# Loading a batch's rows ahead of one expert's weights, and adding masks on TensorE, in a fused attention and expert-mixture kernel

## The chip, the cores and the metric

One core of one Trainium2 chip. The metric is the device time of one execution in microseconds (us). Ratios are the mean time of one kernel's fast runs over the mean of the other's fast runs of the same rounds, so they are not quite the ratio of the medians quoted beside them. A ratio under 1 is faster than the kernel before. Brackets are 95% intervals.

## The reference

```python
# q, k, v: (4 batches, 8 heads, 768 positions, 64); 4 sink positions, window 128
keep = (pos_k < 4) | ((pos_q - pos_k >= 0) & (pos_q - pos_k < 128))
a = softmax(where(keep, q @ k.T / 8, -1e9));  attn = a @ v          # per head
x = attn, heads side by side                                        # (3072, 512)
p = probs / probs.sum(-1)                                           # 4 experts
out = sum_e p[:, e] * (relu(x @ w1[e]) @ w2[e])                     # w1 512x1024, w2 1024x512
```

## The kernel before

The program fixes the order of each engine's instructions beforehand. It keeps a small model of every engine's clock and of the DMA queues (`t`, `landed`, `turned_at`, `xT_at`) and always issues what the model says is ready next. Its figures are the program's own assumptions. So a number in the model moves instructions, and a wrong number puts an instruction that isn't ready in front of others that are.

Row and weight loads go through GpSimd's software DMA queue. They convert float32 to bfloat16 on the way. Transposes are DMAs too, on SyncE's hardware queue. `turn_nat` turns a batch's q and k rows into `qkT` for the scores. `values` turns the attention output `onat` into `xT`, the input of the expert layers.

```python
def sp(*deps, issue=530, takes=600):             # the model of a hardware-queue DMA
    t["sp"] = max([t["sp"], *deps]) + issue
    at = max(t["hw"], t["sp"] + 800)
    t["hw"] = at + takes + max(0.0, min(takes, t["sw"] - at))   # at most twice as long
    return t["hw"] + 900                                        # beside software loads
# ... cut: turn_nat, where the margin (LATE = 2500) is added
turned_at[b, tb] = sp(landed["qk", b, tb], ..., issue=1330, takes=1400) + LATE
# ... cut: values(), batches 1 to 3
nc.sync.dma_start(out=xT[b, g]..., in_=o..., transpose=True)
turned_out = sp(at, issue=1330, takes=1400)
for x in range(NHP):
    xT_at[b, x, g] = turned_out                  # from here on T may be formed
# ... cut: tokens(): four sums T on VectorE from xT, for experts in a seven-product form
```

The first batch's scores are masked in one of two ways. A group below `BIASED` gets a product `ident x low` on TensorE that adds 0 or -32768 ahead of the scores. Any other group has the exponentials multiplied by a 0/1 mask on VectorE (L657).

When the first batch's attention is planned, the rest of the loads are queued: expert 3's first weights, the second batch's rows and values, expert 3's second weights. After a batch's last row transpose GpSimd runs a copy of two columns (`held`), which keeps the next batch's loads from overwriting rows that are still being turned.

The softmax here doesn't subtract the row's maximum and nothing guards it: scores larger than these inputs give would overflow.

## Time and profile before

| | |
|---|---|
| time | 370.87 us, median of 3 runs (370.61 to 371.45) |
| span of the profiled run | 368.9 us |
| TensorE busy | 358.5 us (97%) |
| largest wait of TensorE | 2.47 us, sink scores of the second batch on a row transpose, at 78.4 us |
| granted clock, 79 to 83 us | 0.57 |

In the profile PE is TensorE, DVE VectorE, ACT ScalarE, POOL GpSimd and SP SyncE, and L12 is line 12 of the kernel. A line of a timeline has the start, the duration, the engine, the line, the operation with its tiles, and in brackets how long the engine had idled before it and what ended that.

### The profile page before, as it was taken

How to read it: one execution, taken by the hardware profiler on the slowest of the kernel's cores; microseconds unless marked ns; L12 is line 12 of the kernel's file. 1: busy time of each engine (PE TensorE's matmuls, PEld its weight loads, DVE VectorE, ACT ScalarE, POOL GpSimd, SP SyncE). 2: the span in 40 equal slices, each digit the busy share in tenths (PEclk: the TensorE clock that was granted, in tenths of full speed). 3: DMA queues.
4: the chain of work that ended last, by engine and by line, in shares of the span. 5: the costliest groups of instructions: out<-in, count | busy, mean ns of one | idle time of the engine just before them, and what ended most of it. 6: DMA issues, size and time to landing. Idle time of an engine off the chain costs nothing.

```text
span 368.9 us, 9862 instructions
## 1 busy us (share of the span) xinstructions
PE 358.5 (97%) x4105; PEld 296.9 (81%) x4117; DVE 283.1 (77%) x629; ACT 154.7 (42%) x397; POOL 71.2 (19%) x92
## 2 busy tenths in 40 slices
PE   7899999979999999999999999999999999999996
PEld 3585767637677788898888898899999999999995
DVE  6855985636662899779969979869898988898860
ACT  5854633566556245446445545552103213223110
POOL 8945117304900950010020000000000000000000
PEclk9999999989999999999999999999999999999999
DMA  9999999999999992519692031213002111020011
GB/s 164 172 187 200 210 206 146 148 161 136 137 182 210 200 165 43 85 45 88 129 157 76 15 103 30 44 44 85 16 17 87 30 44 59 16 74 2 2 59 57
DMA packets 117288, 37.20 MB, mean 101 GB/s; under 512 B 100612, under 2 KB 112740, under 8 KB 117244
## 3 DMA queue, kind: packets, MB, share of 16 engines
q0 software_dynamic: 77520, 17.31, 53.5%
q1 hardware_dynamic: 38668, 18.75, 24.6%
q8 instruction: 32, 0.52, 0.6%
q10 hardware_dynamic: 1056, 0.52, 0.5%
q14 instruction: 12, 0.10, 0.1%
HBM read 40.45 MB, written 6.34 MB: 127 GB/s over the span
## 4 chain that ended last, share of the span: by engine, by line
PE 74%; DMA 16%; POOL 4%; DVE 3%; issue 1%; ACT 0%; POOLq 0%; DVEq 0%; SPq 0%
PE acc L1235 29%; PE cps L1081 20%; PE hps L1003 15%; DMA w<-in_moe_w_dram 11%; PE acc L1306 6%; DMA qkT<-qkn 3%; DMA qkn<-in_k_dram 3%; PE sps L623 2%; PE od L689 2%; POOL qkn L191 1%; POOL vx L256 1%; PE od L682 1%; DVE H L1027 1%; POOL w L269 0%; POOL w L279 0%
## 5 line engine op out<-in xcount | busy, mean ns | idle before, releaser
L1003 PE MATMUL hps<-xT,w 128*128 128x256 bf16 x768 | 95.0, 273 | 0.8 <-DMA w<-in_moe_w_dram 0.7
L1003 PEld LDWEIGHTS <-w 128*128 128x128 bf16 x768 | 72.7, 98 | 13.7 <-issue 1.6
L1235 PEld LDWEIGHTS <-H 128*128 128x128 bf16 x600 | 56.0, 98 | 6.4 <-issue 0.8
L648 ACT ACTIVATE aT<-sps 128x512 bf16<-128x512 f32 (+1 forms) x96 | 47.2, 570 | 25.2 <-PE sps L623 25.1
L1081 PEld LDWEIGHTS <-w 128*128 128x128 bf16 x768 | 48.3, 98 | 2.0 <-issue 0.5
L1235 PE MATMUL acc<-w,H 128*128 128x256 bf16 x360 | 48.0, 273 | 0.0
L728 ACT ACTIVATE onat<-od,R 128x64 bf16<-128x64 f32 x144 | 33.4, 322 | 32.1 <-DVE R L716 30.2
L1306 PE MATMUL acc<-w,H 128*128 128x512 bf16 x180 | 45.3, 388 | 0.8 <-issue 0.3
L1100 DVE SCALAR_TENSOR_TENSOR H<-cps,gates 128x512 bf16<-128x512 f32 x57 | 38.6, 683 | 2.2 <-PE cps L1081 1.2
L1016 ACT ACTIVATE H<-hps 128x512 bf16<-128x512 f32 x40 | 23.9, 597 | 35.8 <-PE hps L1003 35.5
L1278 ACT COPY osb<-acc 128x256 f32<-128x256 f32 x36 | 13.5, 374 | 58.2 <-PE acc L1235 56.0
L1027 DVE SCALAR_TENSOR_TENSOR H<-hps,gates 128x512 bf16<-128x512 f32 x44 | 30.0, 685 | 9.3 <-PE hps L1003 9.1
L1306 PEld LDWEIGHTS <-H 128*128 128x128 bf16 x192 | 18.1, 99 | 18.7 <-issue 1.6
L256 POOL DMA_DIRECT2D vx<-in_v_dram x24 | 21.4, 910 | 58.8 <-PE od L689 51.9
L1235 PE MATMUL acc<-wf,H 128*128 128x256 bf16 x240 | 31.9, 273 | 0.0
L1235 PEld LDWEIGHTS <-S 128*128 128x128 bf16 x288 | 27.0, 98 | 3.1 <-issue 0.3
L1081 PE MATMUL cps<-T,w 128*128 128x128 bf16 x384 | 29.3, 219 | 0.0
L1081 PE MATMUL cps<-xT,w 128*128 128x128 bf16 x384 | 29.1, 219 | 0.0
L642 DVE TENSOR_TENSOR aT<-aT,mask 128x1024 bf16<-128x1024 bf16 (+1 forms) x36 | 22.6, 638 | 8.4 <-ACT aT L648 8.4
L1109 ACT COPY cps<-cps 128x512 f32<-128x512 f32 x24 | 13.8, 576 | 33.2 <-PE cps L1081 31.0
L1081 PEld LDWEIGHTS <-vf 128*128 128x128 bf16 x432 | 26.9, 98 | 1.0 <-issue 0.3
L1318 DVE SCALAR_TENSOR_TENSOR osb<-acc,scale_t,osb 128x512 f32<-128x512 f32 x18 | 13.5, 749 | 12.9 <-PE acc L1306 12.0
(116 smaller groups left out, 513.6 us busy)
## 6 DMA issues: line engine op xcount, KB each, us to landing
w<-in_moe_w_dram POOLq DMA_DIRECT2D x7, 1024.0 KB, 16.3
out_dram<-osb SPq DMA_DIRECT2D x23, 256.0 KB
gates<-gate_rows SPq DMA_DIRECT2D x36, 128.0 KB
vx<-in_v_dram POOLq DMA_DIRECT2D x24, 128.0 KB, 7.9
qkn<-in_q_dram POOLq DMA_DIRECT2D x22, 128.0 KB, 7.1
qkn<-in_k_dram POOLq DMA_DIRECT2D x22, 128.0 KB, 7.0
w<-in_moe_w_dram POOLq DMA_DIRECT2D x2, 512.0 KB, 8.1
kraw<-in_k_dram ACTq DMA_DIRECT2D x2, 256.0 KB
```

The lines of the kernel that those rows point to most:

```text
L256: nc.gpsimd.dma_start(out=vx[tb][:, :, 0:D], in_=v[b, :, tb * P:(tb + 1) * P, :].rearrange("h p d -> p h d"),)
L642: nc.vector.tensor_mul(a, a, m[:, None, :].to_broadcast([P, 2, w]))
L648: nc.scalar.activation(out=a[:, ph], in_=sps[ph][:, 0:w], func=AF.Exp, scale=scale)
L728: nc.scalar.mul(o[:, qi, hp, ph * D:(ph + 1) * D], od[:, qi, ph, 0:D], R[:, qi, ph])
L1003: nc.tensor.matmul(h[:, i].rearrange("p (q n) -> p q n", q=2), lhsT=w1_sb[e][:, db, fb * P:(fb + 1) * P], rhs=xT[b, g][:, :, db], start=(i ...
L1016: nc.scalar.activation(out=dst, in_=h, func=AF.Relu)
L1027: nc.vector.scalar_tensor_tensor(out=dst, in0=h, scalar=0.0, in1=gate, op0=ALU.max, op1=ALU.mult,)
L1081: nc.tensor.matmul(y[:, f], lhsT=A[:, d, f * P:(f + 1) * P], rhs=T[:, d], start=(m in ("P1", "P5") and f == 0 and d == 0), stop=(d == 1), ...
L1100: nc.vector.scalar_tensor_tensor(out=dst, in0=src, scalar=0.0, in1=gate, op0=ALU.max, op1=ALU.mult)
L1109: nc.scalar.copy(out=tiles["Y"], in_=y)
L1235: nc.tensor.matmul(x, lhsT=self.operand(b, g, e, m)[:, f], rhs=forms[e][m][:, f], start=(k == 0 and f == 0 and m in (("P1", "P5", "P2") if ...
L1306: nc.tensor.matmul(op, lhsT=H[:, fb // QF, fb % QF, s], rhs=w2_sb[e][:, fb, :], start=(fb == 0), stop=(fb == NFB - 1),)
```

## The change

The intent: the second batch's rows arrive one weight load earlier, and the model assumes that their transposes arrive much later, so that TensorE isn't sent to scores whose transposes are still under way. The masks of the first batch's second group of queries leave VectorE, which is nearly full there; the first group's are products already, and the third group's stay on VectorE.

```diff
-    BIASED = 1
+    BIASED = 2
...
-        turned_at[b, tb] = sp(...) + LATE
+        turned_at[b, tb] = sp(...) + (LATE if b > 1 else 8500)
...
-            loads.append((load_w1, 3))
             for tb in range(NQB):
                 loads.append((load_nat, 1, tb))
                 if tb % 2:
                     loads += [(load_v, 1, (tb - 1,)), (load_v, 1, (tb,))]
-            loads.append((load_w2, 3))
+            loads += [(load_w1, 3), (load_w2, 3)]
```

More of the change, by code (lines that the diff above doesn't have):

```diff
@@ L206, in turn_nat @@
         )
-        turned_at[b, tb] = sp(landed["qk", b, tb], scored_at.get(b - 1, 0.0), issue=1330, takes=1400) + LATE
+        turned_at[b, tb] = sp(landed["qk", b, tb], scored_at.get(b - 1, 0.0), issue=1330, takes=1400) + (LATE if b > 1 else 8500)
         qkn_free.remove(1e12)
```

## The prediction

> **What bounds the kernel now.** I read the page first: which engine is full, and when.
>
> ```profile
> PE 358.5 (97%) x4105; PEld 296.9 (81%) x4117; DVE 283.1 (77%) x629; ACT 154.7 (42%) x397; POOL 71.2 (19%) x92
> ...
> PE   7899999979999999999999999999999999999996
> ...
> PEclk9999999989999999999999999999999999999999
> DMA  9999999999999992519692031213002111020011
> ```
>
> TensorE is the bound almost throughout. Two slices matter: near 74 us PE drops to 7, and just after it, near 80 us, the granted clock drops to 8. DMA is full until about 70 us. So one event at 74 to 83 us costs time, and everything after it is a full TensorE, which passes a gain or a loss on to the end. The second view, waits on TensorE, names what is waited for:
>
> ```profile
> PE sinks L584 <- DMA qkT<-qkn: 2.5, 1, 2.5
> PE acc L496 <- DVE lent L410: 1.4, 1, 1.4
> PE hps L1003 <- DMA w<-in_moe_w_dram: 0.7, 2, 0.5
> PE sps L623 <- DVE qkT L227: 0.4, 1, 0.4
> ```
>
> The largest is one wait of 2.5 us by the second batch's sink scores for a transpose of its rows. The third view, the TensorE timeline around it (start, duration, line, and the idle time before), shows what follows the wait:
>
> ```profile
> 67.52 1.89 PE L1306 MATMUL acc<-w,H 128*128 128x512 bf16 x8
> ...
> 75.25 0.71 PE L689 MATMUL od<-vx,aT 128*128 128x65 bf16 x18
> 78.43 0.29 PE L584 MATMUL sinks<-qkT,ksd 128*32 128x256 bf16 x4 [2.47 <-DMA qkT<-qkn]
> 78.66 0.40 PE L623 MATMUL sps<-qkT 64*128 64x128 bf16 x6
> 78.98 3.21 PE L1306 MATMUL acc<-w,H 128*128 128x512 bf16 x8
> ```
>
> The same eight 512-column products take 1.89 us before the hole and 3.21 us after it. The stretches give the clock (window, its length, PE busy, ..., granted clock, DMA share, GB/s):
>
> ```profile
> 79.00:83.00 4.00, 4.00 (x23) 1.54 (x21) 1.44 (x2) 3.81 (x16) 0.00 (x0) 0.57 1.25 198
> 83.00:90.00 7.00, 6.95 (x82) 5.32 (x80) 3.95 (x8) 5.29 (x15) 1.91 (x3) 1.00 0.93 146
> ```
>
> So 4.00 x (1 - 0.57) = 1.7 us more is lost to a slower clock. The hole costs 2.5 + 1.7 = 4.2 us. Its origin is in the chain of work that ended last, in order of time, and in GpSimd's timeline:
>
> ```profile
> 28.99 27.61 DMA w<-in_moe_w_dram
> ...
> 58.79 9.38 DMA qkn<-in_k_dram
> 68.23 10.07 DMA qkT<-qkn
> ```
>
> ```profile
> 51.75 0.87 POOL L191 DMA_DIRECT2D qkn<-in_q_dram  x1 [4.17 <-DMA w<-in_moe_w_dram]
> 56.88 0.87 POOL L191 DMA_DIRECT2D qkn<-in_k_dram  x1 [4.26 <-DMA w<-in_moe_w_dram]
> ```
>
> Expert 3's first weights, issued at 28.99, land at 56.6 in a full software queue; the second batch's rows come after them, and the transpose that TensorE waits for lands at 68.23 + 10.07 = 78.3. Each weight load that lands frees one issue, and those are 56.88 - 51.75 = 5.1 us apart: one such load holds the queue for 5.1 us.
>
> [...]eight 512-column products in 1.73 us and 24 of 256 columns in 2.62 us.[...]
>
> **The change, part by part.**
>
> *Rows ahead of weights.* In the changed order GpSimd issues the second batch's twelve row loads and six value loads right after expert 2's weights; expert 3's weights come after them. One 5.1 us load leaves the front, so the transposes land about 5.1 us earlier (estimate): the one at 78.3 at about 73.2.
>
> *Wide margin.* It is an entry in the program's own order planning, not a wait. TensorE's order changes only before expert 3's first product; from there to the end the two orders are the same. Ahead of the second batch's sink scores stand 9472 more columns, 3328 of them from the masks (below); the other 6144 are expert 2 work brought forward[...]. The sinks, reached at 75.96 before (end of the last products), are thus reached near 78.5, against an arrival near 73.2: 5 us of slack. The hole and its slow clock should go: **-4.2 us**.
>
> *Masks as products.* Added on TensorE: 8 products of 512 columns, 8 x 0.216 = 1.73 us. The order also drops 3 idle products of 256 columns, 3 x 0.109 = 0.33. Net +1.4 us of TensorE work at 14 to 18 us. That stretch isn't full:
>
> ```profile
> 14.00:18.00 4.00, 3.04 (x41) 1.59 (x40) 3.75 (x8) 4.00 (x9) 4.00 (x6) 1.00 1.22 195
> ...
> 17.88 1.92 PE L1003 MATMUL hps<-xT,w 128*128 128x256 bf16 x16 [0.55 <-DMA w<-in_moe_w_dram]
> ```
>
> TensorE idles 0.41 us for a copy of keys, then 0.55 and 0.17 for expert 0's weights. Those landings stay where they are, so work placed ahead of them fills the gaps: 1.4 - 1.13 = +0.27 us. Removed on VectorE: 8 mask multiplications of 0.42 us (the row of L657: median 420 ns), 3.4 us, just where VectorE is 3.75 of 4.00 busy. The value products wait for scores, then exponential, then mask, so they can start some 0.4 us sooner; worth 0 to -0.6 us. Net of this part: **0, give or take 0.5 us**. Alone it would barely be seen.
>
> **The rivals.**
>
> *The wait moves to expert 3's first weights.* In GpSimd's new order they stand behind a small copy that waits for the second batch's last transpose:
>
> ```profile
> 87.79 0.18 POOL L1388 COPY held<-qkT 128x2 bf16<-128x2 bf16 x1 [16.67 <-DMA qkT<-qkn]
> ```
>
> It ran at 87.8. In the changed kernel it is 5.1 us earlier, and earlier again by 2 to 3 us because expert 3's second weights (1 MB, issued at 70.25, 16.3 us to landing) no longer share the DMA engines with the last transposes: about 80. The load then needs about 1.6 us to start and 5.1 us of queue, and shares with a transpose: landing at 87.5 to 89.5 (estimate). TensorE reached expert 3's first product at about 94.4 (the first 16 of the 24 products from 92.68 are expert 2's, at 0.109), and now 4.2 us earlier, 90.2. The slack is only 1 to 3 us. If it fails, a wait of 1 to 2.5 us comes back, and if it is as long as the old one the slow clock with it: 368.5 to 371. I give this 25%.
>
> *The masks cost their full price.* If the gaps at 14 to 27 us don't absorb the products: +1.4 us, 368.1. Against it speaks that two of the three waits are for a landing. 10%.
>
> *VectorE becomes the bound.* It is busy 10.0 of 10.0 us at 130 to 140. But it is only 2.4 of 10 busy at 110 to 120, and its work falls. When TensorE comes 4 us earlier, VectorE's inputs do too. Unlikely to take more than 0.5 us.
>
> *The hole was hidden anyway.* Against it: from 90 to 352 us TensorE is busy 261.41 of 262.00 us at clock 1.00, with the same order in both kernels. Nothing there can swallow the 4 us unless a new wait appears.
>
> **Range and chances.** 370.87 - 4.2 + 0 = 366.7; the chance of a wait for expert 3's weights adds about 0.25 x 2 = 0.5: **367.2 us**. The low end is both parts at their best with a little more from freed VectorE (365.6); the high end is a new wait of 2 to 3 us (369.8). Faster by over 2% would need 363.4, and there is no idle time for that: 2%. Slower by over 2% would need 378.3, several new holes: 2%. Within 2%: 96%.
>
> **What would show it right or wrong.** Right: the 2.5 us wait of L584 on qkT is gone; the clock is 1.00 throughout 70 to 90 us; expert 3's first product starts near 90; TensorE reaches the first second-layer product within 0.5 us of its 27.15; the mask line L657 runs 8 times, not 16. Wrong: a wait of the first layer's products on a weight DMA near 90 us, or a second dip of the clock; scores in 14 to 18 us that wait for PSUM or ScalarE; a time at or above 370.

The times per product are those of the chain, 1.73 / 8 = 0.216 us for 512 columns and 2.62 / 24 = 0.109 for 256. At that rate the 6144 columns brought forward are 12 x 0.216 = 2.6 us (an estimate), and 75.96 + 2.6 gives the 78.5. The slow clock behind the hole is in the trace: 0.50 from 79.41 to 82.82 us, 3.41 us, after a gap of 2.47. The load's 1.6 us to start is an estimate that fits the same trace, where rows issued at 88.28 on an empty software queue moved their first packets at 89.8.

## More of the kernel before

The prediction shows the lines of the kernel before that matter. One more from that trace turned out to matter, in the view of the tile xT: which instructions waited for its transposes, how long in us and how often.

```profile
  DVE T L1055: 2.1, 1
```

VectorE stood still for 2.1 us before the first sum T, for a transpose `xT`. No TensorE wait followed from it, and the prediction passed it over.

## The result

The changed kernel took 375.4 us (median of 4 runs, 374.11 to 376.0) against 370.74 us: ratio 1.0121 [1.0088, 1.0154]. It is 1.2% slower, and outside the predicted range of 365.6 to 369.8 us.

The page of the changed kernel, the same rows as of before:

```profile
PE 362.1 (97%) x4122; PEld 298.4 (80%) x4122; DVE 277.7 (74%) x620; ACT 155.1 (42%) x398; POOL 71.4 (19%) x92
...
PE   8999999996699999999999999999999999999996
...
PEclk9999999999599999999999999999999999999999
```

The old dent near 74 us is gone. A deeper one lies in the next two slices, 84 to 103 us, with the clock at half in the second of them. The waits on TensorE and its timeline:

```profile
PE hps L1003 <- ACT H L1016: 6.1, 1, 6.1
```

```profile
77.89 0.29 PE L584 MATMUL sinks<-qkT,ksd 128*32 128x256 bf16 x4
```

```profile
88.24 1.91 PE L1003 MATMUL hps<-xT,w 128*128 128x256 bf16 x16
...
96.26 1.86 PE L1003 MATMUL hps<-xT,w 128*128 128x256 bf16 x8 [6.11 <-ACT H L1016]
```

The sink scores now start at 77.89 without a wait, where the prediction said 78.5. The 16 products of expert 2 end near 90, and expert 3's first eight should have followed at once. They start 6.1 us later, and not because of their weights: those had landed at 85.4. They wait for a slot of PSUM, the memory that takes TensorE's results, and ScalarE has to empty it (L1016). The chain that ended last (start, length, what) says what ScalarE waited for:

```profile
79.65 13.32 DMA xT<-onat
...
94.67 0.10 DVE R L716
94.77 0.02 issue
94.80 0.93 ACT onat L728 x4
95.72 0.50 ACT H L1016
```

And VectorE's timeline, the link between the first two:

```profile
85.74 0.17 DVE L716 RECIPROCAL R<-od 128x4 f32<-128x4 f32 x1
92.99 0.29 DVE L1055 TENSOR_TENSOR T<-xT 128x256 bf16<-128x256 bf16 x1 [7.08 <-DMA xT<-onat]
...
94.59 0.17 DVE L716 RECIPROCAL R<-od 128x4 f32<-128x4 f32 x1
```

Read from the top: SyncE issues the transpose `xT` at 79.65 and it lands 13.3 us later. (In the kernel before it was issued at 83.21, and VectorE's wait for it ended at 90.1, after 6.9 us.) VectorE has reached the sum T that reads it and stands for 7.08 us. Behind T in its queue is a reciprocal R. ScalarE needs R for its next work, and behind that work is the ReLU that empties the PSUM slot for which TensorE waits. No single engine is overloaded. One late DMA holds up three engines, because in each of them the needed work stands behind an instruction that waits.

The stretches for the clock (window, length, busy times, granted clock, DMA share, GB/s):

```profile
92.00:96.30 4.30, 0.04 (x1) 0.04 (x1) 1.74 (x6) 1.50 (x6) 2.63 (x4) 0.52 2.64 153
96.30:102.40 6.10, 6.10 (x23) 2.70 (x23) 0.38 (x1) 1.27 (x3) 4.38 (x6) 0.50 2.55 156
```

The half clock (0.52) costs nothing while TensorE is idle (busy 0.04 of 4.30 us). From 96.3 on it costs 6.1 x 0.5 = 3.1 us. The account against the kernel before: first second-layer product reached at 26.67 instead of 27.15, -0.5; old hole gone, -4.2; new hole +6.1 and its slow clock +3.1. The sum is +4.5 us. The profiled spans differ by 373.6 - 368.9 = 4.7.

### The profile page after: what moved, and what is told of

Read it like the earlier page. It is cut to its first block, busy times and chain, and to the rows that moved or that the text cites. A ratio compares the mean times of both kernels' runs of the same rounds, so it can differ in the third digit from the quotient of the medians.

```text
span 373.6 us, 9870 instructions
## 1 busy us (share of the span) xinstructions
PE 362.1 (97%) x4122; PEld 298.4 (80%) x4122; DVE 277.7 (74%) x620; ACT 155.1 (42%) x398; POOL 71.4 (19%) x92
## 4 chain that ended last, share of the span: by engine, by line
PE 87%; DVE 5%; DMA 4%; ACT 3%; issue 1%; DVEq 0%; ACTq 0%
PE acc L1235 29%; PE hps L1003 20%; PE cps L1081 19%; PE acc L1306 9%; DMA xT<-onat 4%; PE sps L623 2%; PE od L689 2%; PE acc L496 2%; ACT onat L728 1%; ACT aT L648 1%; PE od L682 1%; DVE H L1027 1%; DVE aT L642 1%; PE tx L747 1%; PE tr L517 1%
## 5 line engine op out<-in xcount | busy, mean ns | idle before, releaser
L1003 PEld LDWEIGHTS <-w 128*128 128x128 bf16 x768 | 73.4, 98 | 19.6 <-issue 8.2
L1306 PE MATMUL acc<-w,H 128*128 128x512 bf16 x192 | 47.1, 390 | 0.0
L1016 ACT ACTIVATE H<-hps 128x512 bf16<-128x512 f32 x42 | 25.0, 598 | 40.1 <-PE hps L1003 40.0
```

The lines of the kernel that those rows point to most:

```text
L1003: nc.tensor.matmul(h[:, i].rearrange("p (q n) -> p q n", q=2), lhsT=w1_sb[e][:, db, fb * P:(fb + 1) * P], rhs=xT[b, g][:, :, db], start=(i ...
L1016: nc.scalar.activation(out=dst, in_=h, func=AF.Relu)
L1306: nc.tensor.matmul(op, lhsT=H[:, fb // QF, fb % QF, s], rhs=w2_sb[e][:, fb, :], start=(fb == 0), stop=(fb == NFB - 1),)
```

## The experiments

**Theory A**: the loss comes from the order of the loads. Expert 3's weights now run beside the transpose `xT`; it takes 13.3 us, and VectorE, told by the model to expect it early, waits for it with needed work behind. **Rivals**: the mask products cause the wait (B); TensorE would have had to wait for weights or PSUM anyway (C). Further rivals are named with their runs. All runs were correct.

| run | edit | median us | ratio to before |
|---|---|---|---|
| e1 | before + masks as products | 370.65 | 1.0020 [0.9995, 1.0044] |
| e2 | changed, masks back on VectorE | 376.12 | 1.0172 [1.0142, 1.0202] |
| e3, e8, e11 | changed + model told that xT is late | 366.76, 366.80, 367.57 | 0.9913 [0.9885, 0.9940], 0.9902 [0.9884, 0.9920], 0.9925 [0.9899, 0.9951] |
| e4 | before + margin + masks, old load order | 370.03 | 1.0014 [0.9972, 1.0057] |
| e5 | changed, expert 3's weights in 256-byte packets | 367.88 | 0.9928 [0.9901, 0.9955] |
| e6 | e3 with the old narrow margin | 369.52 | 0.9973 [0.9957, 0.9990] |
| e7, e10 | e3 with the masks back on VectorE | 370.03, 369.14 | 0.9985 [0.9964, 1.0006], 0.9952 [0.9925, 0.9980] |
| e9 | e7 + products that nobody reads | 366.40 | 0.9890 [0.9872, 0.9908] |

e1 to e4 ran on one chip together, e5 to e8 together, and e9 to e11 together. The kernel before had medians of 369.44, 370.48 and 370.61 us in these.

### e1 and e2: one part alone

```diff
# e1, against the kernel before
-    BIASED = 1
+    BIASED = 2
# e2, against the changed kernel
-    BIASED = 2
+    BIASED = 1
```

> The kernel before with one edit, the masks of the second group as products (BIASED = 2); loads and margin as before. Theory A (the loss comes from the moved weights: the transpose of the first attention rows, xT, runs beside expert 3's two weight loads, takes 13.3 us, and VectorE, in order, waits for it with work behind it that ScalarE and TensorE need): no new hole near 90 us; the old hole before the sink scores stays, because it ends with a DMA landing at about 78.3 that this edit doesn't move; 370.3 to 371.0 us. Rival B (the products load ScalarE or PSUM and cause the new wait on H L1016): a wait of about 6 us of L1003 on ACT H and 374 to 376 us.

> The changed kernel without its mask part (BIASED = 1): only the loads' order and the margin. Theory A: the new hole of about 6 us at 90 us and the slow clock are there as in the changed kernel, the old hole is gone; 375 to 376.5 us. Rival B: no hole at 90 us, 366 to 367 us.

e1 has no hole near 90 us. Its waits on TensorE still begin with the old one:

```profile
PE sinks L584 <- DMA qkT<-qkn: 2.6, 1, 2.6
```

e2 has the new hole without any mask product, and one wait more:

```profile
PE hps L1003 <- ACT H L1016: 4.7, 1, 4.7
PE hps L1003 <- DMA w<-in_moe_w_dram: 2.3, 1, 2.3
```

B falls: the loss belongs to the loads' order and the margin. The second wait of e2, and why e2 isn't faster than the changed kernel, is taken up below (e7 to e10).

### e3: the transpose stays slow, but VectorE is not sent to wait for it

```diff
-                turned_out = sp(at, issue=1330, takes=1400)
+                turned_out = sp(at, issue=1330, takes=1400) + (10000 if (b, g) == (1, 0) else 0)
```

In the built program this moves four sums T to a later place in VectorE's order, and nothing else on any engine; the two traces agree with that.

> The changed kernel, but the planner is told that the transpose of the second batch's first attention rows lands 10 us later. This leaves every transfer where it is and only moves VectorE's sums T (L1055) behind other work in its queue. Theory A: xT still takes 12 to 14 us from issue to landing, but VectorE no longer waits for it with the reciprocals behind it; no wait of L1003 on ACT H; clock 1.00 at 80 to 100 us; 365.5 to 367.0 us. Rival C (TensorE would have had to wait for expert 3's weights or PSUM anyway): a wait of 4 us or more near 90 us remains, under another name, 372 to 376 us.

366.76 us, ratio 0.9913 [0.9885, 0.9940]. The largest waits on TensorE:

```profile
PE acc L496 <- DVE lent L410: 1.4, 1, 1.4
PE acc L1306 <- issue: 0.3, 2, 0.2
```

VectorE's timeline and the stretch that held the new hole:

```profile
96.82 0.28 DVE L1055 TENSOR_TENSOR T<-xT 128x256 bf16<-128x256 bf16 x1
```

```profile
90.00:100.00 10.00, 9.84 (x89) 6.47 (x88) 4.54 (x13) 6.17 (x13) 3.50 (x4) 1.00 1.64 195
```

The first T runs at 96.8 with no wait, TensorE is busy throughout, and the clock is 1.00. Expert 3's weights and PSUM weren't the cause, so C falls. Nobody waits for `xT` in this kernel, but the DMA views of short stretches show that it stayed slow: it is issued at 80.12, and its packets move on the hardware queue from 83.9 to 92.8 us, so the last one comes 12.7 us after the issue (12.6 in the changed kernel, from 79.65 to 92.2). The place of four 0.3 us sums in one in-order queue accounts for the whole loss: 375.4 to 366.8 us. The result is below the kernel before, as the two later repeats confirm.

### Why the transpose takes 13 us: packets

The DMA view of 80 to 84 us of the kernel before, and of 88 to 91 us of the changed kernel (queue: packets, MB, share). q0 is the software queue, carrying weights; q1 is the hardware queue, carrying transposes.

```profile
q0 software_dynamic: 615, 0.63, 92.3%
q1 hardware_dynamic: 588, 0.15, 28.5%
```

```profile
q0 software_dynamic: 462, 0.47, 92.4%
q1 hardware_dynamic: 458, 0.12, 29.6%
```

The packets are nearly one to one, but a weight packet carries 0.47 MB / 462 = 1 KB and a transpose packet 256 bytes. The transpose gets a fifth of the bytes, 0.12 MB / 3 us = 40 GB/s. At that rate its 0.26 MB (1024 packets) need some 6.5 us. With no weights beside it, in 87 to 88 us of the kernel before, the same queue moved 1129 packets in 1 us.

This rate doesn't account for the whole 13.3 us. Expert 3's first weights come in packets of 2 KB, and while they pass (440 packets, 0.90 MB, in 79 to 83.5 us of the changed kernel) the transpose moves nothing: its first packet comes 3.9 us after the issue. Why it starts only then isn't shown; beside row loads, in the kernel before, the first row transpose of the second batch needed 3.3 us (58.65 to 61.9). In 84 to 88 us only 374 of its packets move, partly because both queues slow down (9 to 34 GB/s near 87 us, below).

e5 tests whether the packets' size matters. It loads expert 3's weights in twelve pieces of 128 columns, so that their packets are 256 bytes too (1348 packets, 0.34 MB, in 82 to 87 us). Apart from the twelve issues every engine's order is the changed kernel's, T's early place included.

```diff
+            m = P if e == 3 else n
+            for c in range(i * n, (i + 1) * n, m):
+                nc.gpsimd.dma_start(out=w1_sb[e][:, :, c:c + m], in_=moe_w1[e][:, c:c + m]...)
# and the same for the second weights
```

> The changed kernel, every engine's order kept, but expert 3's weights are loaded in twelve pieces of 128 columns, so that a packet carries 256 bytes instead of 2 KB and 1 KB. Theory A, with its cause for the slow transpose[...]: beside the weights the transpose now moves about as many bytes as they do, xT lands within 4 to 7 us of its issue instead of 13.3, VectorE's wait before its first T falls from 7.1 us to under 1.5, the wait of L1003 on ACT H is gone; 365.8 to 367.5 us. Rival E (the transpose is slow because all weights' bytes go first, or because SyncE or VectorE is late): xT still lands after 10 us or more, and the hole stays; 373 to 376 us.

367.88 us. VectorE's largest single wait for `xT` fell from 7.1 to 3.1 us, and TensorE's hole is what is left:

```profile
92.83 1.03 PE L1009 MATMUL hps<-xT,w 128*128 128x256 bf16 x8 [2.18 <-ACT H L1022]
```

(Lines are shifted by six. The profile fell on a run of 369.00 us, slower than the median.) VectorE's first T starts at 89.55, which puts the landing 9.4 us after the issue at 80.14. A's direction holds: with small packets the hole shrinks from 6.1 to 2.2 us and the slow clock is gone. The size doesn't: 9.4 us is above the 4 to 7 expected, and E's bound of 10 is only just missed. The first packet comes 1.9 us after the issue instead of 3.9, and the packets then take 5.9 us instead of 8.7. That packet size alone does this isn't shown: the twelve issues also spread the weights over 9.5 us on GpSimd (76.94 to 86.40, against 76.50 to 78.13), and weights that come at a slower pace may leave the transpose more room. This rival wasn't tested. While the transpose is under way all queues together move only 14 to 49 GB/s in two spells of some 0.4 us each. Slack spells are in the changed kernel (9 to 34 GB/s near 87 us) and in e3 (9 to 32 GB/s) as well. Their cause is open.

### e4 and e6: the order or the margin?

```diff
# e4: the kernel before with BIASED = 2 and
-        turned_at[b, tb] = sp(...) + LATE
+        turned_at[b, tb] = sp(...) + (LATE if b > 1 else 8500)
# e6: e3 with the reverse of that line
```

> The kernel before with the margin and the masks, but expert 3's first weights stay ahead of the rows. Theory A: the planner puts the sink scores about 9 us later than before, after the transposes that land at 78.3, so the old hole goes without moving a load; xT runs beside one weight load only, not two; 366 to 368 us if VectorE's place for T is late enough, with a wait of at most 3 us if not. Rival D (only moving the loads can remove the old hole): a wait of L584 on qkT of 2 us or more stays, 370 us or more.

> The kernel of e3 with the old narrow margin for the second batch's rows (2500 instead of 8500): tells whether the order of the loads alone removed the old hole. The sink scores then stand 16384 columns earlier in TensorE's order[...], so TensorE comes to them near 71.5 us; the transpose they need lands about 5.1 us earlier than in the kernel before, near 73.2 (estimate). Theory A: a wait of L584 on qkT of 1 to 2.5 us is back, perhaps with a slow clock; 368 to 370 us. Rival F (the margin does nothing): no such wait, the time of e3, 366.3 to 367.2 us.

e6's 16384 columns at the measured 0.216 us for 512 are 6.9 us (an estimate).

In e4 the first sink scores, put later, start at 83.1 without a wait. The second ones, of the last third of the batch, then wait at 90.5:

```profile
90.48 0.40 PE L584 MATMUL sinks<-qkT,ksd 128*32 128x256 bf16 x4 [2.77 <-DMA qkT<-qkn]
```

A slow clock follows: the eight 256-column products behind the wait take 1.89 us, against 1.03 ahead of it. The last row transposes of this kernel run beside expert 3's second weights, with 154 packets of each queue in 83 to 84 us, so a like sharing falls on another transpose. A's "at most 3 us of wait" held, its 366 to 368 us did not. D's figures came true, a wait of L584 of over 2 us and 370 us, but not its reason: the old hole is gone without moving a load, and this wait is another. The profiled run took 372.31 us; the others vary from 369.07 to 370.64.

e6, with the rows early but the narrow margin, brings a wait back at the place expected (sink scores at 73.4 us):

```profile
PE sinks L584 <- DMA qkT<-qkn: 1.1, 1, 1.1
```

369.52 against 366.80 us for e8 on the same chip. The clock stayed at 1.00, so the 2.7 us are this wait and several of 0.4 to 0.8 us beside it, of which the 0.8 is for expert 0's first weights and not the margin's. Both parts are needed: the order makes the transposes early, the margin puts the work that needs them late. (e4 lacks e3's correction for `xT`, but its VectorE doesn't wait for `xT` at that place.)

### e7 to e11: what the mask products are worth

> The kernel of e3 without the masks as products (BIASED = 1): the price of that part where nothing else waits. Theory A: within 0.6 us of e3 either way, because the products fill waits for expert 0's weights, which come back as 0.5 to 0.8 us of waits of L1003 on the weights; 366.2 to 367.3 us. Rival G (the products cost their full 1.4 us of TensorE): 1.0 to 1.5 us faster than e3, 365.2 to 365.8 us.

> The kernel of e3 once more, as the base for e6 and e7 on the same chip: 366.2 to 367.0 us, no wait on TensorE over 0.5 us after the first products, clock 1.00 throughout.

e8 came out as expected. e7 differs from e3 by `BIASED = 1` only, and both expectations missed. Five of its six runs took 368.7 to 370.8 us with a mean clock of 0.991 to 0.995; one took 366.84, and the profile fell on that one. A mean clock of 0.995 over some 367 us is 1.8 us lost. That fits one spell at half like that of the kernel before (3.41 us, 1.7 lost). e2's profile shows where such a spell can come from. First TensorE's timeline of e2, then its stretch:

```profile
19.32 2.47 PE L1003 MATMUL hps<-xT,w 128*128 128x256 bf16 x16 [2.27 <-DMA w<-in_moe_w_dram]
```

```profile
20.50:24.00 3.50, 3.50 (x40) 3.06 (x39) 2.65 (x8) 0.60 (x1) 1.02 (x2) 0.51 1.24 208
```

Expert 0's first weights landed at 17.8 us in the one profile of the kernel before, but at 18.1 to 19.4 in the others. Without mask products TensorE is there at about 17.3. It then waits up to 2.3 us (e2) and may lose 1.7 us more to the clock (3.50 x 0.49 in e2).

```diff
# e9: e7, with idle products in the places of the mask products
+        if b == 0 and g == 1:
+            idle_products(acc[1], 2)
```

> The kernel of e3 with the masks back on VectorE, and with eight products of 512 columns that nobody reads in the places of the mask products: TensorE has the same work ahead of expert 0's first products, VectorE keeps its eight multiplications. It asks why e7, without mask products, was slower in five of its six runs. Theory H (the mask products only fill TensorE's wait for expert 0's first weights, which land at 17.8 to 19.4 us from run to run, and so keep its clock): 366.3 to 367.5 us, as with the masks; no slow clock at 20 us. Rival I (what counts is VectorE's relief of 3.4 us): 369 to 370.5 us, as e7.

> e7 once more, for a second profile: its first fell on the fastest of its runs. Theory H: most runs at 369 to 371 us; where the profile falls on such a run, L1003 waits 1 to 2.5 us for expert 0's first weights near 17 to 19 us and the clock is at half for one window of 3.4 us near 20 us. Rival I: no such wait and no slow clock, the time lost by values products that wait for VectorE.

> e3 a third time, as the base on this chip: 366.3 to 367.1 us, clock 1.00.

e9 took 366.40 us, ratio 0.9890; e10, without mask or idle products, 369.14 and 0.9952. Products that nobody reads do as well as the masks, so what counts is TensorE being occupied, not VectorE's relief: H holds. They didn't make the weights land earlier (expert 0's first product starts at 18.77 in e9, at 18.67 in e10); what they saved is the clock (means of 0.999 and 1.000 in e9's four runs, 0.995 in three of e10's four). e10's profile again fell on its fastest run (367.44), with the wait but no slow clock:

```profile
18.67 0.50 PE L1003 MATMUL hps<-xT,w 128*128 128x256 bf16 x3 [1.34 <-DMA w<-in_moe_w_dram]
```

Its other three runs, at clock 0.995, were 1.7 to 2.0 us slower, which is the price of one such spell. That the spell lies at 20 us in those unprofiled runs is inferred from e2, not shown. e11 scatters more than e3 and e8 (366.29 to 368.23) and its median misses the expected 366.3 to 367.1, for a reason that the runs don't show. The mask products, then, are worth (0.9985 - 0.9902) and (0.9952 - 0.9925), 0.8% and 0.3%, some 1 to 3 us; the intervals of the second pair overlap. In the kernel before they are worth nothing that the runs show (e1). This fits the old hole's end, a DMA landing that was not moved by what was gained ahead of it: the sink scores start at 78.76 in e1 and at 78.43 before. No run separates the two.

**The version to keep** is e3: both parts of the change and the corrected model, 0.9902 to 0.9925 of the kernel before in three sets of rounds.

## Why the prediction was wrong

- **The old hole, -4.2 us: mechanism right, size a little large.** Sink scores without a wait at 77.89 (predicted 78.5), clock 1.00 there. Where the new hole is gone too, the gain is 2.8 to 3.6 us (e3, e8, e11 by their ratios), 3.8 by the profiled spans of e3 and the kernel before (365.1 and 368.9). One profile hid that the slow clock isn't in every run: 6 of the 25 later runs of the kernel before have a mean clock of 1.000.
- **Expert 3's first product near 90.2, weights as the risk: position right, risk wrong.** TensorE was ready for it at 90.0. The weights landed at 85.4, earlier than the estimated 87.5 to 89.5: the small copy ahead of them ran at 76.27, not at about 80.
- **The step that failed** is in the rivals: the load "shares with a transpose". It counted what the sharing does to the load and not what it does to the transpose. The sum had no term for `xT`. It measured 13.3 us instead of 6.9, and through VectorE +6.1 us of hole and +3.1 us of slow clock. The before trace already showed 615 and 588 packets but 0.63 against 0.15 MB in 80 to 84 us; that wasn't applied to the next transpose in line. It had also read the DMA row as full until about 70 us; the row's first fifteen slices are all 9, which is up to 138 us.
- **"From there to the end the two orders are the same"** (from expert 3's first product on) was read on TensorE only. The place of T in VectorE's order, just ahead of a reciprocal, decided the outcome (e3). VectorE's 2.1 us wait there in the kernel before was the warning: the change brought two weight loads beside a transpose for which an engine already waited.
- **"Nothing there can swallow the 4 us unless a new wait appears"** was true, and the new wait appeared. The 25% was put on the wrong DMA.
- **Masks, 0 give or take 0.5 us: mechanism right, size wrong.** They do fill the wait for expert 0's weights, but that wait was read from one profile (0.55 us) in which the weights happened to land early. Across runs it is up to 2.3 us, with the clock behind it (0.51 in 20.5 to 24 us of e2), and the part is worth 1 to 3 us once nothing later hides it. VectorE's relief, counted as up to 0.6 us, isn't what pays (e9).

## What to carry to other kernels

Before moving a large load, list every small transfer on another queue that will now run beside it, and work out its new time from the packet counts and bytes of a stretch where the two already overlap. Then see which in-order engine reaches that transfer's reader first and what stands behind it: the late operand mattered here through the queue behind it, and moving its reader back was enough (e3, 375.4 to 366.8 us). A wait measured in one profile is a sample. If it ends with a DMA landing, look at other profiles before calling work placed ahead of it free or useless.

## What the traces show of the queues and the clock

- In three stretches with 1 KB weight packets and a transpose both under way, their packets were nearly one to one: 462 and 458 in 88 to 91 us of the changed kernel, 461 and 455 in the same stretch of e3, 615 and 588 in 80 to 84 us of the kernel before. In the first of these the transpose with its 256-byte packets got 0.12 of 0.59 MB. Other stretches differ: beside 2 KB packets the counts were 440 and none (79 to 83.5 us of the changed kernel), beside row loads 3935 and 1130 (67 to 72 us).
- One transpose took 13.3 us from issue to landing, 3.9 us of it before its first packet, while weights of 2 KB and then 1 KB packets passed, and 9.4 us beside 256-byte packets (e5).
- Idle gaps of 2.27 us (e2), 2.47 us (before) and 2.77 us (e4) were followed by half clock, while 2.18 us (e5), 1.34 us (e10) and 1.1 us (e6) were not. In the changed kernel the clock fell at 92.20, within the gap of 6.11 us. The slow spells of the two kernels lasted 3.41 us (79.41 to 82.82, before) and 10.24 us (92.20 to 102.44, changed), three times as long. In the 3.41 us ahead of the drop TensorE was busy for 0.98 us (before) and 1.37 us (changed). In the changed kernel the clock stayed at half after 95.61 to 99.02 us, in which TensorE was busy for 2.76 us, and was full again after 99.02 to 102.44, in which it was busy throughout. Where the limits lie isn't shown.
- Slack spells of under 1 us, with all queues together at 9 to 49 GB/s, were seen while a transpose ran beside weights (changed kernel, e3, e5). Their cause is open.
